# Keys and first query halves projected in one step for pairs 16 to 31, and 27 low parts computed on GpSimd

## The chip, the cores and the metric

The kernel runs on one core of a Trainium2 chip. The metric is the device time of one execution in microseconds (us). TensorE (PE in the profile) multiplies, VectorE (DVE), ScalarE (ACT) and GpSimd (POOL) do elementwise work, and every bulk transfer is issued from SyncE (SP). Results of TensorE land in eight banks of PSUM, each 512 float32 wide in 128 partitions; DVE and ACT read them from there.

## The reference

Attention with positive random features, followed by a gated feed-forward layer. There are 8 batches of 8 heads with 576 tokens and head width 64:

```python
def phi(x):
    proj = einsum('bhsd,df->bhsf', x, w_phi)              # 64 -> 128 features
    proj = proj - max(abs(proj), axis=-1)
    return concatenate([exp(proj), exp(-proj)], axis=-1)  # 256 features
q_p, k_p = phi(q), phi(k)
kv  = einsum('bhsf,bhsd->bhfd', k_p, v);  z = sum(k_p, axis=2)
x   = einsum('bhsf,bhfd->bhsd', q_p, kv) / (einsum('bhsf,bhf->bhs', q_p, z) + 1e-6)
g   = x @ w_gate                                          # 4608 x 512 @ 512 x 1536
out = (g / (1 + exp(-g)) * (x @ w_val)) @ w_out           # back to 4608 x 512
```

All tensors are float32. Two heads make a pair, so the attention has 32 pairs (0 to 31), four to a batch.

## The kernel before

**Feed-forward.** The 4608 tokens are twelve chunks of 384, the 1536 hidden columns twelve tiles f of 128. Every operand of these matmuls is split into a high part and a low part (the rest), and a product is the sum of three matmuls: high by high, high by low, low by high. `first(c, f)` makes one hidden tile of chunk c from the tokens, `second` multiplies a hidden tile into three blocks of outputs. A hidden tile ("middle tile", `m` in the trace) is either used at once or stored and fetched again later. Before `second` uses it, `parts` splits it: ACT copies the high part (`s4`, into a buffer `hh`) and another engine subtracts it from the tile to get the low part (`s5`). Chunk 0 is computed first while the weights are still being split on DVE, ACT and POOL (`weight_piece`, tiles `shared`, `ahead`, `w_big`, `w_hi`, `w_lo`). Then come chunks 1 to 3, during which POOL also makes sums of weights (`sums`, tile `s`), and chunks 4 to 11 go two at a time by a Strassen-like scheme (`strassen`, line 1145). The list `more_low` is empty until chunk 3 has been through `first`; `ring_on` is empty until chunks 1 to 3 are done.

**Attention.** `attention(i, rank)` adds the work of pair i: the keys are projected (lines 544 and 547: 8 matmuls into two banks and one, the tail, into a third), DVE takes the largest magnitude and subtracts it (lines 555, 561), ACT takes both exponentials (line 566), and 72 matmuls sum keys by values (lines 583, 576; called kv below). From pair 12 on the queries are projected in two halves of 288 columns, two matmuls each (line 689, called q below), ACT copies them out (line 694), DVE turns them and finds their maxima. Line 734 and line 743 then make denominators and numerators (called dn below).

**What sets the order.** All of this is a list of steps with costs, dependencies and ranks. `Plan.run` plays the list through with these costs and emits the instructions in the order in which the play starts them, so every engine's queue is written out beforehand. A step can take banks (`take`) and give them back (`give`); it starts in the play only when as many banks are free. The products of the feed-forward form one chain on PE. Attention work on PE of pairs 12 and up is ordered by due times, brought forward by `MARGIN`. [...] Where the play finds nothing ready for PE, it emits a filler matmul of 128 by 256 on zeros (`idle`, line 1342 before the first tile of the feed-forward, line 1344 after). PE steps have a mode: `rows` (64-row matmuls: key and query projections), `quarters` (32-column matmuls: kv and dn) and `whole`; once in a mode, the play goes on with steps of that mode that are ready.

## Time and profile before

| | us |
|---|---|
| Median of 3 runs | 1177.37 (1176.76 to 1177.45) |
| Profiled execution | 1175.58 |
| Span of the profiled execution | 1173.8 |
| PE busy in the span | 1161.7 (99%) |
| DVE busy | 829.4 (71%) |
| ACT busy | 594.7 (51%) |
| POOL busy | 139.1 (12%) |

[...] Matmuls overlap: the busy time of one is longer than the distance from its start to the start of the next, so what a step costs on PE is read from starts. The timeline merges consecutive instructions of one kind into a row with a count; the float32 matmuls of the attention appear in it as two passes each.

### The profile page before, as it was taken

Reading aid. Unit: us, or ns where it says so; the run is one execution under the profiler, and the core shown is the slowest. Engines: PE = TensorE matmul, PEld = TensorE weight load, DVE = VectorE, ACT = ScalarE, POOL = GpSimd, SP = SyncE. Lnnn points to the kernel's source line nnn. Section 1 sums busy time; section 2 is a strip of 40 time slices with the busy share of each in tenths; the row PEclk is TensorE's granted clock in tenths of the full one; section 3 lists DMA queues with packets and bytes.
Section 4 is the critical chain, followed back from the end, with each engine's and each line's share of the span. In section 5 each row is a group of like instructions: output and inputs, shape, how many; then the busy total and the mean of one; then the engine's idle time right before and its main releaser. Section 6 shows DMA issues by size and latency. Waiting matters only on the chain.

```text
span 1173.8 us, 29868 instructions
## 1 busy us (share of the span) xinstructions
PE 1161.7 (99%) x11684; PEld 995.1 (85%) x11684; DVE 829.4 (71%) x1509; ACT 594.7 (51%) x1325; POOL 139.1 (12%) x143
## 2 busy tenths in 40 slices
PE   9999999999999999999999999999999999999998
PEld 7777799999988877888887789887799878899986
DVE  7989999999646787768889475788645785534441
ACT  6887643333533657546665544566533654423332
POOL 1223210000032131101010001010001010001100
PEclk9999999999999999999999999999999999999999
DMA  5646789997698799897887689788779868789764
GB/s 169 179 123 180 247 267 302 308 294 256 221 335 283 243 325 365 301 307 233 275 290 240 219 281 303 231 250 249 260 231 302 255 198 276 276 272 306 253 217 160
DMA packets 217644, 301.68 MB, mean 257 GB/s; under 512 B 62752, under 2 KB 122272, under 8 KB 217504
## 3 DMA queue, kind: packets, MB, share of 16 engines
q1 hardware_dynamic: 217344, 299.71, 79.4%
q8 instruction: 92, 1.51, 0.5%
q14 instruction: 48, 0.39, 0.1%
q10 hardware_dynamic: 160, 0.07, 0.0%
HBM read 221.05 MB, written 78.64 MB: 255 GB/s over the span
## 4 chain that ended last, share of the span: by engine, by line
PE 90%; DVE 5%; DMA 1%; issue 1%; ACT 1%; SPq 1%; POOL 0%; DVEq 0%; ACTq 0%; POOLq 0%
PE work L382 39%; PE work L1145 31%; PE work L583 4%; PE work L743 4%; PE work L544 3%; PE work L689 2%; PE work L576 1%; PE work L662 1%; PE work L734 1%; DMA m<-h_dram 1%; PE work L1344 1%; PE work L739 1%; PE work L640 1%; PE work L1342 1%; DVE kp L561 1%
## 5 line engine op out<-in xcount | busy, mean ns | idle before, releaser
L382 PE MATMUL work<-w_hi,hh 128*128 128x512 f32 x468 | 183.0, 399 | 0.8 <-ACT osb L969 0.5
L1167 DVE TENSOR_TENSOR m<-m,work 128x384 f32<-128x384 f32 x144 | 78.6, 553 | 117.6 <-ACT m L1164 68.0
L382 PE MATMUL work<-w_hi,m 128*128 128x512 f32 x396 | 156.6, 396 | 0.0
L382 PE MATMUL work<-xh,w_big 128*128 128x384 f32 x384 | 132.0, 344 | 1.7 <-DVE m L911 1.7
L375 DVE TENSOR_TENSOR m<-m,hh 128x384 fp32r<-128x384 f32 x132 | 74.4, 570 | 79.7 <-ACT hh L938 75.6
L382 PE MATMUL work<-xl,w_big 128*128 128x384 f32 x384 | 128.6, 335 | 0.0
L938 ACT CAST hh<-m 128x384 fp32r<-128x384 f32 x144 | 72.9, 512 | 109.6 <-PE work L382 62.9
L375 POOL TENSOR_TENSOR m<-m,m 128x384 f32<-128x384 f32 x48 | 58.0, 1208 | 590.7 <-DVE m L1172 423.9
L1145 PE MATMUL work<-tb,stream_xh 128*128 128x384 f32 x618 | 115.7, 338 | 0.1
L1145 PEld LDWEIGHTS work<-tb,stream_xh 128*128 128x128 f32 x618 | 107.1, 188 | 5.6 <-issue 3.5
L382 PEld LDWEIGHTS work<-w_hi,hh 128*128 128x128 f32 x468 | 87.8, 188 | 26.7 <-issue 4.5
L1164 ACT COPY m<-work 128x384 f32<-128x384 f32 x144 | 67.9, 474 | 68.8 <-PE work L1145 66.8
L566 ACT ACTIVATE kp<-kp 128x512 f32<-128x512 f32 x128 | 77.7, 627 | 34.0 <-DVE kp L561 32.9
L1171 ACT ACTIVATE m<-m 128x384 f32<-128x384 f32 x96 | 45.4, 517 | 89.1 <-DVE m L1167 89.0
L382 PEld LDWEIGHTS work<-w_hi,m 128*128 128x128 f32 x396 | 74.4, 188 | 18.2 <-DVE m L375 0.3
L1145 PE MATMUL work<-tb,stream_xl 128*128 128x384 f32 x468 | 87.8, 337 | 0.1
L1145 PEld LDWEIGHTS work<-tb,stream_xl 128*128 128x128 f32 x468 | 81.1, 188 | 3.3 <-issue 1.5
L382 PEld LDWEIGHTS work<-xh,w_big 128*128 128x128 f32 x384 | 72.3, 188 | 8.8 <-issue 3.8
L1145 PE MATMUL work<-tb,tb 128*128 128x384 f32 x408 | 77.6, 337 | 0.0
L583 PEld LDWEIGHTS work<-vf,kp 128*32 128x32 f32 x4096 | 61.9, 109 | 16.3 <-issue 12.5
L375 POOL TENSOR_TENSOR s<-s 128x256 f32<-128x256 f32 x48 | 40.9, 853 | 278.4 <-DMA s<-w_dram 221.6
L382 PEld LDWEIGHTS work<-xl,w_big 128*128 128x128 f32 x384 | 72.2, 188 | 1.0
(142 smaller groups left out, 2390.0 us busy)
## 6 DMA issues: line engine op xcount, KB each, us to landing
stream_xh<-wv_dram SPq DMA_DIRECT2D x103, 256.0 KB, 4.0
h_dram<-m SPq DMA_DIRECT2D x124, 192.0 KB, 3.9
m<-h_dram SPq DMA_DIRECT2D x124, 192.0 KB, 4.3
w_lo<-wlo_dram SPq DMA_DIRECT2D x80, 256.0 KB, 4.6
stream_xl<-wv_dram SPq DMA_DIRECT2D x78, 256.0 KB, 4.0
tb<-wv_dram SPq DMA_DIRECT2D x77, 256.0 KB, 4.0
stream_w_lo<-wv_dram SPq DMA_DIRECT2D x52, 256.0 KB, 3.8
stream_xl<-wlo_dram SPq DMA_DIRECT2D x48, 256.0 KB, 3.7
```

The costliest lines, as they stand in the source:

```text
L375: (nc.gpsimd if on == "POOL" else nc.vector).tensor_tensor(out=o, in0=a, in1=b, op=op)
L382: nc.tensor.matmul(o, l, r, start=a, stop=z)
L544: nc.tensor.matmul(work[plan.bank["k", i, h]][:, t * NF:(t + 1) * NF], kin[rows(h)[0], t * P:(t + 1) * P], wst[rows(h)[0]], start=True, st ...
L566: nc.scalar.activation(kpv[:, :m2, s], kpv[:, :m2, 1], AF.Exp, scale=-1.0 if s else 1.0)
L583: nc.tensor.matmul(ps_kv()[r, (2 * s + h) * VD:(2 * s + h + 1) * VD], kpv[:, t, s, r], vf[:, t, h], start=t == 0 and h + s == 0, stop=False)
L689: nc.tensor.matmul(work[plan.bank[keys[h]]][:, :SH], wst[rows(h)[0]], qin[jq][rows(h)[0], c], start=True, stop=True)
L743: nc.tensor.matmul(o[at:at + 32], kvs[j][:, k * P + at:k * P + at + 32], features(k, at // D, c), start=first_ and k == 0, stop=k == 1)
L938: s4 = add("ACT", act(CH), lambda: nc.scalar.copy(hh[b], th(j)), [made, hid_free[b]], FIRST)
L1145: nc.tensor.matmul(o(), l, r, start=begin and k + m == 0, stop=k + m == 3, skip_group_check=True)
L1164: return j, into(j, add("ACT", act(CH), lambda: nc.scalar.copy(th(j), src()), after, FIRST))
L1167: return add("DVE", dve(CH), lambda: vec.tensor_tensor(out=th(j), in0=th(j), in1=src(), op=ALU.add), after, FIRST)
L1171: s1 = into(t, add("ACT", act(CH), lambda: nc.scalar.activation(th(t), th(j), AF.Tanh, scale=0.5), [ready], FIRST))
```

## The change

For pairs 16 to 31 (`joint`) one step on PE projects the keys, the tail of the keys and the first half of the queries. It takes four banks together: two for the keys, two for the queries, and the tail lies in the first query bank behind the query's 288 columns. That bank is given back only when both ACT has copied the queries and DVE has subtracted from the tail. The second half of the queries stays a step of its own and waits for the joint one. `MARGIN` goes from 65e3 to 75e3. In `parts`, the low part of a tile is made on POOL and no longer on DVE as long as `more_low` and `ring_on` are empty, which is so for 27 tiles: the twelve of chunk 0 and the first fifteen of chunks 1 and 2.

```diff
-MARGIN = 65e3
+MARGIN = 75e3
...
+        joint = i >= 16
...
+            tail_bank, tail_at = (("k", i, 2), slice(0, NF)) if not joint else (("q", i, 0, 0), slice(SH, SH + NF))
...
                 if both or not early:
-                    nc.tensor.matmul(work[plan.bank["k", i, 2]][:, :NF], kin[:D, 4 * P:], wst[:D], start=True, stop=True)
+                    nc.tensor.matmul(work[plan.bank[tail_bank]][:, tail_at], kin[:D, 4 * P:], wst[:D], start=True, stop=True)
+                if joint:
+                    for h in range(2):
+                        nc.tensor.matmul(work[plan.bank["q", i, h, 0]][:, :SH], wst[rows(h)[0]], qin[jq][rows(h)[0], :SH],
+                                         start=True, stop=True)
...
-                kproj = add("PE", (4 if early else 5) * pe32(NF), project, [*k_in, last.get(("kp", i - 1, 0))], rank,
-                            take=[("k", i, n) for n in range(2 if early else 3)], mode="rows")
+                kproj = add("PE", (4 if early else 5) * pe32(NF) + (pe32(SH) if joint else 0), project, [
+                    *k_in, last.get(("kp", i - 1, 0)), *((*q_in, *use("qx"), last.get(("qy", 3 * i - 1))) if joint else ())], rank,
+                            take=[("k", i, n) for n in range(2 if early or joint else 3)] + ([("q", i, h, 0) for h in range(2)] if joint else []), mode="rows")
...
-            ksub = add("DVE", dve(n), centre, [kmax, last.get(("kp", i - 1, g))], rank, give=key)
+            ksub = add("DVE", dve(n), centre, [kmax, last.get(("kp", i - 1, g))], rank, give=None if both and joint else key)
...
-                pj = add("PE", pe32(SH), project, [*q_in, *use("qx"), last.get(("qy", 3 * i - 1))], rank, take=keys, mode="rows")
+                pj = add("PE", pe32(SH), project, [*q_in, *use("qx"), last.get(("qy", 3 * i - 1)), *([kproj] if joint else [])], rank, take=keys, mode="rows") if part or not joint else kproj
...
+            if joint:
+                add("PE", 1, lambda: None, [copies[0][0], ksub], -2.0, give=("q", i, 0, 0))
...
-        s5 = pair_op("DVE2", CH, low, lambda: th(j), lambda: hh[b], ALU.subtract, [s4], FIRST)
+        s5 = pair_op("POOL" if not ring_on and not more_low else "DVE2", CH, low, lambda: th(j), lambda: hh[b], ALU.subtract, [s4], FIRST)
```

**PE, the projections of pair 17, between products of chunk 3.** Before, both halves of its queries are one stretch (four matmuls of line 689), followed by 18 filler matmuls and the dn of an earlier pair:

```order
L382 MATMUL work_135<-w_hi_79,m_5658 128x512
L689 MATMUL work_137<-qin,wst 128x288
L689 MATMUL work_134<-qin,wst 128x288
L689 MATMUL work_133<-qin,wst 128x288
L689 MATMUL work_130<-qin,wst 128x288
L1344 MATMUL work_132<-idle 128x256 x18
L734 MATMUL work_131<-num,ones 32x288 x2
L734 MATMUL work_131<-den,ones 32x288 x2
L743 MATMUL work_131<-qe_108,kvs_104 32x64 x4
```

In the changed kernel the same pair's step ends with the last matmuls of the keys, the tail (line 551) and two query matmuls (line 554), the tail and a query half in one bank:

```order
L548 MATMUL work_133<-wst,kin 128x128
L548 MATMUL work_131<-wst,kin 128x128
L551 MATMUL work_130<-wst,kin 128x128
L554 MATMUL work_130<-qin,wst 128x288
L554 MATMUL work_136<-qin,wst 128x288
L382 MATMUL work_134<-w_hi_79,hh_122 128x512
L382 MATMUL work_134<-w_lo_85,hh_122 128x512
L382 MATMUL work_134<-w_hi_79,m_5602 128x512
```

The products of the same weight tile (`w_hi_79`) now follow directly, without filler between.

**DVE, in the weight phase, behind one hidden tile of chunk 0** (the row that writes it is the first; `ahead` and `shared` are pieces of weights). Before, DVE makes the tile's low part two instructions later:

```order
L914 TENSOR_TENSOR m_3211<-m_3211,work_131 128x384
L375 TENSOR_TENSOR ahead<-shared_129,w_big_71 128x512
L375 TENSOR_TENSOR hh_122<-m_3211,hh_120 128x384
L409 TENSOR_SCALAR shared_128<-shared_128 128x512
L411 TENSOR_SCALAR shared_128<-shared_128 128x512
L413 SCALAR_TENSOR_TENSOR shared_129<-shared_127,shared_128 128x512
L416 TENSOR_SCALAR shared_128<-shared_129 128x512
```

Now:

```order
L925 TENSOR_TENSOR m_3205<-m_3205,work_131 128x384
L416 TENSOR_SCALAR shared_128<-shared_129 128x512
L418 SCALAR_TENSOR_TENSOR shared_128<-shared_126,shared_128 128x512
L375 TENSOR_TENSOR shared_129<-shared_129,shared_128 128x512
L409 TENSOR_SCALAR shared_128<-shared_128 128x512
L411 TENSOR_SCALAR shared_128<-shared_128 128x512
L375 TENSOR_TENSOR ahead<-shared_129,w_big_71 128x512
```

The row with `hh` is gone from DVE, and rows on weights follow one another.

**POOL, from the end of the weights to the sums of weights.** Before, after the last piece of weights nothing stands in POOL's queue until the sums (`s`):

```order
L375 TENSOR_TENSOR ahead<-shared_129,w_hi_75 128x512
L375 TENSOR_TENSOR shared_129<-shared_129,shared_128 128x512
L375 TENSOR_TENSOR ahead<-shared_129,w_big_70 128x512
L375 TENSOR_TENSOR s_4110<-s_4110 128x256 x4
L375 TENSOR_TENSOR s_4111<-s_4111 128x256 x4
```

Now the low parts (`hh` for chunk 0, `m` for chunks 1 and 2) stand there, some of them behind sums that wait for their own load:

```order
L375 TENSOR_TENSOR hh_123<-m_4027,hh_121 128x384
L375 TENSOR_TENSOR m_4133<-m_4133,hh_120 128x384
L375 TENSOR_TENSOR m_4138<-m_4138,hh_121 128x384
L375 TENSOR_TENSOR m_4145<-m_4145,hh_122 128x384
L375 TENSOR_TENSOR m_4152<-m_4152,hh_123 128x384
L375 TENSOR_TENSOR s_4185<-s_4185 128x256 x4
L375 TENSOR_TENSOR s_4186<-s_4186 128x256 x4
L375 TENSOR_TENSOR m_4376<-m_4376,hh_120 128x384
L375 TENSOR_TENSOR s_4185<-s_4185 128x256 x2
L375 TENSOR_TENSOR m_4422<-m_4422,hh_121 128x384
```

27 rows with low parts have come to POOL in all, and none has left it.

## Rows read from the trace of the kernel before

**Rows 1.** The page: busy time of PE with its share of the span and its instructions, and the chain of work that ended last, by engine.

```profile
PE 1161.7 (99%) x11684; PEld 995.1 (85%) x11684; DVE 829.4 (71%) x1509; ACT 594.7 (51%) x1325; POOL 139.1 (12%) x143
...
PE 90%; DVE 5%; DMA 1%; issue 1%; ACT 1%; SPq 1%; POOL 0%; DVEq 0%; ACTq 0%; POOLq 0%
```

**Rows 2.** What PE waited for, longest first: us in total, times, longest.

```profile
PE work L382 <- DVE m L911: 1.7, 2, 1.2
PE work L1339 <- POOL vl L357: 1.6, 1, 1.6
```

**Rows 3.** Filler matmuls after the first tile, grouped by line: count, busy us, mean ns.

```profile
L1344 PE MATMUL work<-idle 128*128 128x256 f32 x99 | 14.9, 287 | 0.0
```

**Rows 4.** Timeline of PE around steps in `rows` mode: start and duration in us, line, count. First one half of a pair's queries alone, then both halves together, then the keys of a pair, each with the matmul before and behind it.

```profile
363.37 0.34 PE L382 MATMUL work<-xh,w_lo1v 128*128 128x384 f32 x1
363.63 0.76 PE L689 MATMUL work<-qin,wst 64*128 64x288 f32 x4
364.32 0.44 PE L382 MATMUL work<-xh,w_big 128*128 128x384 f32 x1
...
427.76 1.24 PE L689 MATMUL work<-qin,wst 64*128 64x288 f32 x8
428.93 0.74 PE L1344 MATMUL work<-idle 128*128 128x256 f32 x4
...
434.04 0.40 PE L382 MATMUL work<-w_hi,m 128*128 128x512 f32 x1
434.37 1.16 PE L544 MATMUL work<-wst,kin 64*128 64x128 f32 x16
435.37 0.38 PE L547 MATMUL work<-wst,kin 64*128 64x128 f32 x2
435.68 0.50 PE L382 MATMUL work<-w_hi,hh 128*128 128x512 f32 x1
```

**Rows 5.** Timeline of PE around steps in `quarters` mode: kv alone, dn alone, and dn and kv together, first instruction of each and the first one behind it.

```profile
378.93 2.02 PE L583 MATMUL work<-vf,kp 128*32 128x65 f32 x128
...
381.32 0.44 PE L382 MATMUL work<-xh,w_big 128*128 128x384 f32 x1
...
391.43 0.44 PE L734 MATMUL work<-num,ones 128*32 128x288 f32 x2
...
394.00 0.45 PE L382 MATMUL work<-xh,w_big 128*128 128x384 f32 x1
...
417.00 0.44 PE L734 MATMUL work<-num,ones 128*32 128x288 f32 x2
...
421.82 0.44 PE L382 MATMUL work<-xh,w_big 128*128 128x384 f32 x1
```

**Rows 6.** Timeline of PE at the two longest filler runs, near the end of chunk 3, with the instruction behind each; then ACT's copy of the high parts for the products behind the second run (two copies merged).

```profile
472.80 2.40 PE L1344 MATMUL work<-idle 128*128 128x256 f32 x18
475.13 0.44 PE L734 MATMUL work<-num,ones 128*32 128x288 f32 x2
...
481.21 2.18 PE L1344 MATMUL work<-idle 128*128 128x256 f32 x17
483.23 0.40 PE L382 MATMUL work<-w_hi,hh 128*128 128x512 f32 x1
...
480.61 0.93 ACT L938 CAST hh<-m 128x384 fp32r<-128x384 f32 x2
```

**Rows 7.** Busy time by stretch of 15 us: length, then PE, PEld, DVE, ACT, POOL busy us (instructions), granted clock, DMA share, GB/s.

```profile
425.00:440.00 15.00, 14.82 (x103) 10.75 (x104) 10.84 (x18) 6.44 (x15) 3.18 (x5) 1.00 1.00 335
...
455.00:470.00 15.00, 15.00 (x199) 12.15 (x198) 11.43 (x18) 11.24 (x20) 0.72 (x1) 1.00 1.01 360
```

**Rows 8.** The same view in the weight phase, two stretches of one weight tile each.

```profile
201.00:217.30 16.30, 16.30 (x92) 15.26 (x91) 15.61 (x31) 6.37 (x13) 0.00 (x0) 1.00 0.89 292
217.30:233.50 16.20, 16.20 (x104) 15.22 (x103) 14.94 (x28) 5.29 (x9) 0.00 (x0) 1.00 0.91 306
```

**Rows 9.** DVE's groups by line with their mean ns, first from 90 to 180 us, where POOL ran 17 instructions, then from 180 to 270 us, where it ran none.

```profile
L411 DVE TENSOR_SCALAR shared<-shared 128x512 uint32<-128x512 uint32 x11 | 8.0, 724 | 0.2
L409 DVE TENSOR_SCALAR shared<-shared 128x512 f32<-128x512 f32 x11 | 5.8, 530 | 0.5 <-ACT shared L408 0.5
L375 DVE TENSOR_TENSOR hh<-m,hh 128x384 fp32r<-128x384 f32 x3 | 2.6, 874 | 0.0
...
L411 DVE TENSOR_SCALAR shared<-shared 128x512 uint32<-128x512 uint32 x16 | 6.8, 423 | 0.2
L409 DVE TENSOR_SCALAR shared<-shared 128x512 f32<-128x512 f32 x16 | 6.8, 423 | 1.9 <-ACT shared L408 1.9
L375 DVE TENSOR_TENSOR hh<-m,hh 128x384 fp32r<-128x384 f32 x5 | 2.8, 553 | 0.3 <-ACT hh L938 0.3
```

**Rows 10.** POOL's group of the same shape as a low part (another product of tiles), count, busy us, mean ns; and the first sums in POOL's timeline with the idle time before them.

```profile
L375 POOL TENSOR_TENSOR m<-m,m 128x384 f32<-128x384 f32 x48 | 58.0, 1208 | 590.7 <-DVE m L1172 423.9 <-DMA h_dram<-m 64.3 <-issue 36.5
...
321.31 7.33 POOL L375 TENSOR_TENSOR s<-s 128x256 f32<-128x256 f32 x8 [165.75 <-DMA s<-w_dram]
```

**Rows 11.** The first low part of chunks 1 and 2 on DVE, and the matmul on PE that uses it.

```profile
316.43 0.56 DVE L375 TENSOR_TENSOR m<-m,hh 128x384 fp32r<-128x384 f32 x1 [0.34 <-ACT hh L938]
...
318.76 0.39 PE L382 MATMUL work<-w_hi,m 128*128 128x512 f32 x1
```

More of the change, by code (lines that the diff above doesn't have):

```diff
@@ L536, in attention, with project @@
             key = ("k", i, g)
+            tail_bank, tail_at = (("k", i, 2), slice(0, NF)) if not joint else (("q", i, 0, 0), slice(SH, SH + NF))
             view = lambda key=key, n=n: work[plan.bank[key]][:, :n].rearrange("p (t f) -> p t f", f=NF)
-            def project(t0=t0, t1=t1, key=key, heads=heads, both=both):
+            if both:
+                view = lambda tail_bank=tail_bank, tail_at=tail_at: work[plan.bank[tail_bank]][:, tail_at].rearrange("p (t f) -> p t f", f=NF)
+            def project(t0=t0, t1=t1, key=key, heads=heads, both=both, tail_bank=tail_bank, tail_at=tail_at):
                 projected.append(1)
@@ L690, in project @@
                                          start=True, stop=True)
-                pj = add("PE", pe32(SH), project, [*q_in, *use("qx"), last.get(("qy", 3 * i - 1))], rank, take=keys, mode="rows")
+                pj = add("PE", pe32(SH), project, [*q_in, *use("qx"), last.get(("qy", 3 * i - 1)), *([kproj] if joint else [])], rank, take=keys, mode="rows") if part or not joint else kproj
                 for h in range(2):
                     copies[h].append(add("ACT", act(SH), lambda h=h, c=c, key=keys[h]: nc.scalar.copy(
-                        qx[j][:, h, c], work[plan.bank[key]][:, :SH]), [pj, *use("qx")], rank, give=keys[h]))
+                        qx[j][:, h, c], work[plan.bank[key]][:, :SH]), [pj, *use("qx")], rank, give=keys[h] if h or part or not joint else None))
+            if joint:
+                add("PE", 1, lambda: None, [copies[0][0], ksub], -2.0, give=("q", i, 0, 0))
             last["qin", i] = pj
```

## Prediction

> **What bounds the kernel now.** I read the page first: PE is busy for 1161.7 us of a span of 1173.8, and 90% of the chain that ended last is work on PE [rows 1]. What PE waited for comes next: the longest sum is 1.7 us [rows 2]. So there is hardly a wait to remove. The time is the sum of what PE executes, and a change pays by shortening that queue: fewer instructions, fewer fillers, fewer changes between the modes. The printed order says how many of each there are, and starts in PE's timeline say how long each takes. Third, I looked for stretches in which another engine only just keeps up, since fillers hide such waits. There are two. In the weight phase DVE works 15.61 of 16.30 us and 14.94 of 16.20 [rows 8]. Near the end of chunk 3 the transfers run at a share of 1.00 with 335 to 360 GB/s [rows 7].
>
> **Query and key steps, late pairs.** One query half alone occupies PE from 363.63 to 364.32, 0.69 us; two halves together take 427.76 to 428.93, 1.17 us, so the second costs 0.48. Keys with their tail take 434.37 to 435.68, 1.31 us [rows 4]. The joint step isn't in the trace. From below it costs 1.31 + 0.48 = 1.79 us, if the query half joins as a second half does; from above 1.31 + 0.69 = 2.00, if nothing is saved. I take 1.80, because both cases in the rows are one uninterrupted stretch in the same mode. Before, the order has 31 key steps alone, 28 query halves alone and 6 doubles; now 15, 24 and none, and 16 joint steps. That is 16 x 1.80 - 16 x 1.31 - 4 x 0.69 - 6 x 1.17 = -1.9 us (+1.3 with the upper end). Entering such a stretch from an ordinary matmul costs about 0.09 us more (363.37 to 363.63 is 0.26 where the usual distance is 0.17; 434.04 to 434.37 is 0.33 for 0.23) [rows 4]. I count 97 entries into `rows` or `quarters` stretches in both orders, so this term is zero.
>
> **kv and dn.** The joint steps use all the banks that the Strassen part leaves, so other steps are cut apart. kv alone takes 378.93 to 381.32, 2.39 us; dn alone 391.43 to 394.00, 2.57; both in one stretch 417.00 to 421.82, 4.82 [rows 5]. A cut costs 2.39 + 2.57 - 4.82 = 0.14 us. For pairs 12 and up 12 joined stretches become 9: +0.4 us. In the early pairs the order has four more cuts, in kv, dn and query steps. At 0.14 to 0.2 us, estimated from the same difference, and with slightly more for the transposes between them, that is +0.8 us.
>
> **Fillers.** There are 99 after the first tile before [rows 3] and 68 now. In a run one takes (483.23 - 481.21) / 17 = 0.119 us [rows 6]; the mean of 287 ns in the group counts overlapping time and would be wrong here. 31 x 0.119 = -3.7 us. The sum is -1.9 + 0.4 + 0.8 - 3.7 = -4.4 us.
>
> A filler that goes is worth its time only if PE would have had work. Most of those that go stand near the end of chunk 3: 40 of the 99 stand between 428 us and the Strassen part, and 16 are left in the same part of the chain of products. The rows tell how much was a real wait. The second run lasts from 481.21 to 483.23, but the copy of the high part for the next product ends at 480.61 + 0.93 = 481.54 [rows 6]. So at most 0.33 of its 2.02 us was needed. The first, 472.80 to 475.13, is followed by dn and not by a product; for it I can only say that between nothing and all of 2.33 was needed. Needed in the two runs: 0.33 to 2.66 of 4.35 us, 8 to 61%. On the 24 x 0.119 = 2.9 us that go here this gives back 0.2 to 1.8 us. I take 0.8, nearer to the run whose end I can see.
>
> **Low parts on GpSimd.** On DVE one costs 0.55 us when POOL is idle [rows 9]; on POOL an instruction of that shape takes 1.21 us [rows 10], 0.65 later at the user. The least cover that I found is at 316.43: the part ends at 316.99 and PE uses it at 318.76, 1.8 us later [rows 11]. So 0.65 is hidden. In chunks 1 and 2 the parts now stand in POOL's queue behind sums that wait for a load, and behind these the next parts wait; the sums' loads move ahead a little in SP's queue too, so I cost this at zero, and without that cover a late load would hold a part by several us.
>
> In the weight phase POOL was idle for 165.75 us up to 321.31 [rows 10], so there's room. But DVE gets slower beside POOL. With POOL at work the shift on line 411 takes 724 ns instead of 423, line 409 takes 530 instead of 423, the low part 874 instead of 553 [rows 9]: 11 x 0.30 + 11 x 0.11 + 3 x 0.32 = 5.5 us over 17 POOL instructions, 0.32 each. Eight of chunk 0's tiles fall in the stretch from 185 us where DVE only just keeps up, five of them up to 270 us [rows 9]. Each takes 0.55 off DVE and puts on between nothing and 1.21 (DVE held for the whole instruction), so DVE's work there changes by -4.4 to +5.3 us; at 0.32 it is 8 x (0.32 - 0.55) = -1.8. Against that the order brings attention work of DVE forward into this stretch. I take zero for PE and keep +5.3 as the upper end.
>
> [...]
>
> **Sum.** -4.4 + 0.8 = -3.6 us. The profiled execution goes from 1175.58 to 1172.0 (span 1173.8 to 1170.2); it lies 1.8 under the median of the runs, so against the median of 1177.37 I forecast 1173.8.
>
> **The rivals.**
> 1. *The fillers covered waits.* PE's queue gets shorter, but transfers at a share of 1.00 [rows 7] and DVE in the weight phase set the pace, and what was filler becomes idle time in front of line 382. For it: rows 7 and 8. Against it: the filler run that outlasted its data by 1.7 us. Then the 3.7 us come back: -0.7 us, 1176.7.
> 2. [...] Place: the weight phase, 185 to 316 us, where POOL was idle. Each of eight low parts meets a DVE instruction with two inputs and holds it for 1.21 us, DVE falls behind by 5.3 us, and some three us of attention work that now stand there (an estimate: the rows that the order adds, most of them of 0.3 to 1.3 us) can't be absorbed. Price +5.3 + 3.0 - 1.3 (the PE work that came with it) = +7.0, so -4.4 + 7.0 = +2.6: 1180.0. It decides when a low part costs DVE over about 1.2 us; the rows show 0.32.
> 3. *The joint step waits for banks.* It needs four at once, and in the Strassen part only four exist for attention. The second half comes 15 to 33 ordinary matmuls behind it in the printed order, and the tail's bank needs DVE to be done. If DVE is late by half a us at each of 16 pairs, PE stands 8 us: 1181.8. Against it: PE's longest waits name no line of the attention [rows 2], though there the tail had a bank of its own.
> 4. *More gain.* The wait of 1.7 us on line 911 [rows 2] goes as well since DVE has 0.55 less per tile, and no filler was needed: -4.4 - 1.7 = -6.1, 1171.3.
>
> **How the numbers follow.** Forecast 0.52, with a range of its own of 1171.5 to 1176 (the joint step's upper end and the two ends of what fillers give back, and a us for waits that fall elsewhere in a new order). Rival 1 has 0.20, rival 2 0.12, rival 3 0.07, rival 4 0.09. A measurement of this kernel tells about 0.2%, 2.35 us, from no change. Faster by more: nine tenths of the forecast, all of rival 4 and a little of rival 1, 0.58. Within: most of rival 1 and the rest of the forecast, 0.23. Slower: rivals 2 and 3, 0.19. The range is 1169.5 to 1180: below it only rival 4 with more of PE's waits gone, above it rival 3 and the worse part of rival 2.
>
> **What would show it.** Right: 68 fillers in the group of line 1344, with a busy time near 10 us; joint steps that last about 1.80 us from the first key matmul to the next ordinary matmul; query halves alone at 0.69; idle sums on PE no longer than before; low parts of `hh` and `m` in POOL's groups at about 1.2 us. Wrong: idle time before line 382 or 1145 of some us, released by POOL (rival 2 or a part behind a late sum), by DVE's lines 561 or 555 (rival 3) or by transfers (rival 1); or lines 409 and 411 at a mean far over 423 ns between 180 and 270 us.

## The result: 0.57% slower, and the profile after

The changed kernel takes 1183.44 us (median of 8 runs, 1179.74 to 1185.81), the kernel before in the same comparison 1176.72 (8 runs, 1173.89 to 1179.85): a ratio of 1.0057, 95% interval 1.0044 to 1.0071. The forecast was 1173.8 in a range of 1169.5 to 1180.0. The profiled execution took 1179.74 us (span 1177.9), against 1175.58 before. It is the fastest of the eight: the loss that its trace can explain is 4.2 us, the loss of the medians is 6.7.

The page of the changed kernel: span, busy time of each engine, the queues of kind `instruction`, and the chain that ended last.

```profile
span 1177.9 us, 29815 instructions
PE 1157.9 (98%) x11653; PEld 989.5 (84%) x11653; DVE 819.0 (70%) x1482; ACT 594.7 (50%) x1325; POOL 163.7 (14%) x170
...
q8 instruction: 92, 1.51, 0.5%
q14 instruction: 48, 0.39, 0.1%
...
PE 92%; DVE 3%; DMA 2%; issue 1%; SPq 1%; ACT 1%; DVEq 0%; ACTq 0%
```

PE is busy 3.8 us less than in [rows 1], in a span 4.1 us longer. So PE stands more. What it waited for (sum in us, times, longest):

```profile
PE work L585 <- issue: 3.8, 4, 1.6
PE work L1156 <- issue: 2.7, 1, 2.7
PE work L382 <- DVE m L922: 2.4, 3, 1.0
PE work L745 <- issue: 1.7, 1, 1.7
PE work L1350 <- POOL vl L357: 1.6, 1, 1.6
PE work L754 <- issue: 1.4, 1, 1.4
PE work L1156 <- DVE m L1178: 1.0, 1, 1.0
```

Line 922 is line 911 of before, where [rows 2] have 1.7 us, and line 1350 is line 1339, with 1.6. The wait on line 1178 is new. What stands out are the four rows whose releaser is "issue": PE waits for nothing that the profile shows, for 9.6 us. They stand at three unrelated steps: kv, the Strassen part, dn. The kernel before has two such rows, which [rows 2] leave out:

```profile
PE work L576 <- issue: 1.2, 2, 0.9
PE work L544 <- issue: 0.5, 1, 0.5
```

The terms of the prediction did come out. The group of late fillers, which answers to [rows 3]:

```profile
L1355 PE MATMUL work<-idle x68: 274/282/384, 206.0 to 1122.3; 128*128 128x256 f32 x68
```

And a joint step in PE's timeline (start, duration, tile, shape), which answers to [rows 4]:

```profile
433.94 1.16 PE L548 MATMUL work<-wst,kin 64*128 64x128 f32 x16
434.94 0.27 PE L551 MATMUL work<-wst,kin 64*128 64x128 f32 x1
434.94 0.51 PE L554 MATMUL work<-qin,wst 64*128 64x288 f32 x1
435.05 0.27 PE L551 MATMUL work<-wst,kin 64*128 64x128 f32 x1
435.16 0.65 PE L554 MATMUL work<-qin,wst 64*128 64x288 f32 x3
435.74 0.50 PE L382 MATMUL work<-w_hi,hh 128*128 128x512 f32 x1
```

From 433.94 to 435.74 it takes 1.80 us, as forecast, and all 16 joint steps take 1.79 or 1.80. So the loss isn't in the steps that the change makes. It lies in stand-stills like these two, in the timeline of the changed kernel (in brackets the idle time before the row and its releaser):

```profile
389.91 2.02 PE L592 MATMUL work<-vf,kp 128*32 128x65 f32 x128
391.75 0.62 PE L585 MATMUL work<-vl,kpt 128*32 128x130 f32 x14
393.79 0.41 PE L585 MATMUL work<-vl,kpt 128*32 128x130 f32 x2 [1.42 <-issue]
...
586.39 0.68 PE L1156 MATMUL work<-tb,stream_w_lo1v 128*128 128x384 f32 x3
589.75 1.14 PE L1156 MATMUL work<-tb,stream_w_lo1v 128*128 128x384 f32 x3 [2.67 <-issue]
```

The kv step of 389.91 stops after 14 of the 16 last matmuls; a row of six equal matmuls of line 1156 is cut in the middle. Nothing in the program separates the first part from the second. What separates them is their number. I counted all the trace's records of PE's queue in order of time (weight loads, matmuls and the few records of semaphores; without these the remainder below does not come out) and set beside each stand-still the last packet of queue q8 (kind `instruction`, 92 packets of 16 KB):

```
number of    = 256 x  PE starts  next     gap    packet of q8        next start
the record            last at    start           from      to       after the packet
 4800        18 + 192   110.06    111.84   1.79   109.52   110.48    1.36
 6080        23 + 192   156.67    157.14   0.47   154.76   155.74    1.40
 9664        37 + 192   392.10    393.80   1.70   391.55   392.47    1.32
14016        54 + 192   586.75    589.75   3.01   587.50   588.38    1.37
15296        59 + 192   640.80    642.76   1.95   640.47   641.51    1.25
17600        68 + 192   769.94    772.06   2.12   769.66   770.61    1.46
18880        73 + 192   823.73    824.62   0.89   822.33   823.27    1.35
```

All seven lie at a number that leaves 192 over 256, and PE goes on 1.25 to 1.46 us after a packet has come. Together they are 11.93 us. The kernel before has three of this kind, 2.44 us in all. I take the places to be the edges of the pieces in which PE's program is fetched, 256 instructions in 16 KB. Both figures are in the trace (1.51 MB in 92 packets; stand-stills at distances that are multiples of 256). In order of time, each of the trace's 92 such numbers after the first has its own packet among the 92, and at none of these 91 does PE pass sooner than 1.25 us after the end of that packet, also where it doesn't stand.

In this trace, how long PE stands follows from two things: how fast it runs through the piece before the edge, and when the packet for the next piece starts. In the median a packet starts 0.7 us after PE has passed the edge before it and lasts 1.0 us. Five of the seven pieces were run through in 1.8 to 2.3 us. The other two (the stand-stills at 586.75 and 640.80) took 3.1 and 3.5 us, but their packets started 3.8 and 3.2 us after the edge before; why so late the trace doesn't say.

The longest has a sequel. Busy time per stretch of the changed kernel (columns: stretch, length, busy us and instructions of PE, PEld, DVE, ACT, POOL, granted clock, DMA share, GB/s):

```profile
583.00:586.70 3.70, 3.70 (x152) 3.25 (x151) 3.70 (x6) 2.25 (x7) 1.21 (x1) 1.00 0.91 292
586.70:589.80 3.10, 0.43 (x4) 0.11 (x2) 2.83 (x9) 0.43 (x2) 0.00 (x0) 1.00 1.10 368
589.80:593.40 3.60, 3.60 (x34) 2.56 (x38) 2.61 (x2) 0.00 (x0) 0.00 (x0) 0.53 0.59 184
593.40:597.00 3.60, 3.60 (x27) 2.14 (x20) 0.49 (x1) 1.41 (x5) 0.00 (x0) 1.00 0.04 9
```

PE stands, and then its granted clock is 0.5 of full speed for 3.41 us by the trace's clock records (590.0 to 593.4), so some 1.7 us of work are lost (an estimate: half of the 3.41). The first row shows the other side: before the stand-still PE ran 152 matmuls in 3.70 us, while the transfers were at 0.91 to 1.10 of their share.

The account of the profiled executions: the sum as forecast -3.6, edges 11.93 - 2.44 = +9.5, the clock +1.7, which makes +7.6; measured +4.2. The other 3.4 us went the right way, and the experiments come back to them. Of the 2.5 us by which the medians differ more, part may be the clock: its mean is 0.998 of full speed in the profiled execution and in one other, and 0.996 or 0.997 in the other six. A mean lower by 0.001 to 0.002 over 1178 us is 1 to 2.4 us (an estimate from these means; there is no trace of those executions).

### The profile page after: what moved, and what is told of

Read it like the earlier page. It is cut to its first block, busy times and chain, and to the rows that moved or that the text cites. A ratio compares the mean times of both kernels' runs of the same rounds, so it can differ in the third digit from the quotient of the medians.

```text
span 1177.9 us, 29815 instructions
## 1 busy us (share of the span) xinstructions
PE 1157.9 (98%) x11653; PEld 989.5 (84%) x11653; DVE 819.0 (70%) x1482; ACT 594.7 (50%) x1325; POOL 163.7 (14%) x170
## 3 DMA queue, kind: packets, MB, share of 16 engines
q8 instruction: 92, 1.51, 0.5%
## 4 chain that ended last, share of the span: by engine, by line
PE 92%; DVE 3%; DMA 2%; issue 1%; SPq 1%; ACT 1%; DVEq 0%; ACTq 0%
PE work L382 39%; PE work L1156 30%; PE work L754 5%; PE work L592 5%; PE work L548 3%; PE work L698 1%; PE work L585 1%; PE work L750 1%; PE work L745 1%; PE work L671 1%; PE work L649 1%; PE work L554 1%; DMA kin<-in_kT_dram 1%; DMA shared<-in_wv_dram 1%; PE work L1353 1%
## 5 line engine op out<-in xcount | busy, mean ns | idle before, releaser
L375 DVE TENSOR_TENSOR m<-m,hh 128x384 fp32r<-128x384 f32 x117 | 65.4, 566 | 76.6 <-ACT hh L949 73.0
L1156 PEld LDWEIGHTS work<-tb,tb 128*128 128x128 f32 x408 | 70.7, 188 | 4.5 <-issue 3.2
```

What stands on the lines that cost most here:

```text
L375: (nc.gpsimd if on == "POOL" else nc.vector).tensor_tensor(out=o, in0=a, in1=b, op=op)
L1156: nc.tensor.matmul(o(), l, r, start=begin and k + m == 0, stop=k + m == 3, skip_group_check=True)
```

## Experiments

**Theory.** PE stands where a burst of short matmuls (kv: 288 instructions in 2.4 us) runs it over the edge of a piece before the next piece is there. The change moved the instructions against the edges, and more bursts fell on one. **Rivals.** The joint step waits for banks, or DVE and POOL hold each other up in the weight phase (the prediction's rivals 3 and 2): then the place of the edges doesn't matter, and the changed kernel stays at its 1183 us wherever they lie.

**Moving the edges alone.** A number of tiny matmuls on zeros ahead of PE's first filler moves all later instructions against the edges and leaves the order of every queue as it is. PE has only fillers there anyway (20 of line 1339, from 1.57 to 6.01 us in the kernel before). 52 matmuls are 208 instructions; 18 are 72, 40 are 160, 54 are 216 and 64 are 256.

```diff
+    padded = []
     def nothing():
         if not begun and not projected:
+            if not padded:
+                padded.append(1)
+                zeros = idle.bitcast(F32)
+                for n in range(52):
+                    nc.tensor.matmul(ps(("gv", 1, 0), VD)[quarters[n % 4]], zeros[:, :32], zeros[:, :VD], start=True, stop=True)
```

The changed kernel with 208 instructions:

> The changed kernel with 208 more instructions in front of PE's first filler matmul (52 matmuls of 32 by 65 on zeros, in four instructions each), everything else in the same order. Theory (code fetch): PE's program comes in pieces of 256 instructions; in the changed kernel's trace PE stood six times, 11.5 us in all, each time at an instruction whose number is 192 modulo 256, and went on 1.2 to 1.5 us after a piece of 16384 bytes had landed. Moving the program by 208 instructions puts the bursts of attention matmuls elsewhere against the edges; by the times between edges in the trace some 4 to 8 us of the standing goes, the padding itself costs at most 1.5 us at the start: 1175 to 1180 against 1183.4. [...]

Measured: 1172.33 us (1169.92 to 1177.12), ratio to before 0.9963 (0.9944 to 0.9983). Eleven us less than without padding, and under the theory's own range.

With 72:

> The changed kernel with 72 more instructions in front (18 of the same matmuls). Theory (code fetch): by the times between edges this is near the worst place, 12 edges fall where PE runs through a piece in under 2.9 us instead of 6: 6 to 14 us slower than the changed kernel, 1189 to 1197. [...]

Measured: 1172.15 us (1171.1 to 1174.36), ratio 0.9965 (0.995 to 0.9979). The number that I had expected to be the worst place is as good as the other. So my forecast of single edges is no use: it went by how fast PE runs through a piece alone, and the start of the packet varies as well (in this kernel up to 5.8 us after the edge before); that the place decides stands. In PE's timeline of this kernel the kv step that stopped at 391.75 goes through:

```profile
389.31 2.02 PE L592 MATMUL work<-vf,kp 128*32 128x65 f32 x128
391.15 0.63 PE L585 MATMUL work<-vl,kpt 128*32 128x130 f32 x16
391.71 0.76 PE L698 MATMUL work<-qin,wst 64*128 64x288 f32 x4
```

The kernel before with 216 and with 160 instructions:

> The kernel before with 216 more instructions in front. Theory (code fetch): no edge is left where PE runs through a piece in under 2.9 us (4 now), so the kernel before gets 0 to 3 us faster less at most 1.5 us of padding: 1173 to 1177. Rivals, which speak of the change alone: 1177 to 1178.5.

Measured: 1180.45 us (1178.98 to 1183.12), ratio 1.0029 (1.0012 to 1.0046). A miss: I had expected a gain. The edges sum to 5.87 us in its profile. The longest stands in these rows of PE's timeline, and by the trace's clock records 6.8 us at 0.5 of the full clock begin in it (504.7 to 511.5; another 3.4 us of this execution, from 95.1, follow a wait of PE away from the edges):

```profile
500.28 2.00 PE L583 MATMUL work<-vf,kp 128*32 128x65 f32 x122
505.91 0.44 PE L583 MATMUL work<-vf,kp 128*32 128x65 f32 x6 [3.63 <-issue]
```

> The kernel before with 160 more instructions in front. Theory (code fetch): ten edges instead of four where PE runs through a piece in under 2.9 us: 6 to 14 us slower than before, 1183 to 1191, though no order, wait or engine changed. Rivals: padding alone, 1177 to 1178.

Measured: 1180.57 us (1180.17 to 1183.15), ratio 1.0035 (1.0022 to 1.0048), edges 7.95 us. That is some 2.5 us under the range of the theory and as much above that of the rivals. At both other places the kernel before is 3 to 4 us slower, so it owed as much to a lucky place of its edges.

**The control.** A whole piece of padding brings every instruction back to its place within a piece.

> The changed kernel, order of every queue as it is, with 64 tiny matmuls (256 instructions, one whole piece of PE's program) ahead of PE's first filler. Theory (PE stands where a burst of small matmuls runs it over the edge of a 256-instruction piece before the next has come): every later instruction lies where it lay within its piece, so the stand-stills come back: 1182 to 1186 us, edge gaps summing to 10 to 13 us in the profile, at the same steps as in the changed kernel (L585, L1156, L754, L745). Rival (the padding as such helps, for instance because PE is busy earlier, whatever its length): as with 72 and 208 instructions, 1171 to 1174 us.

Measured: 1184.56 us (1179.36 to 1186.36), ratio 1.0064 (1.0048 to 1.0081); edges 13.31 us, at the lines expected. The same padding code, three lengths: 1172, 1172 and 1184.6. So it isn't the padding that helps, it's the place. All four forecasts of single places had missed; this one, which asks for no length of a stand-still, holds.

**The cost by itself.** 512 tiny matmuls in one go.

> The same with 512 tiny matmuls (2048 instructions, eight pieces) in one go: the disputed cost measured by itself. Theory: within the burst PE stands once in every 256 instructions, at numbers that leave 192 over 256, with each stand-still 0.5 to 3 us and the next matmul 1.2 to 1.5 us after the end of a 16 KB packet of the instruction queue; the piece is run in some 2 us and comes in some 3, so that eight pieces take some 24 us rather than 16. The rest of the program keeps its phase, so it has the changed kernel's gaps. Rival (PE's code is there ahead of time and the stand-stills are a wait that the profile does not name): the burst runs through without a gap over 0.3 us. Total some 1185 to 1205 us, of no use by itself.

Its timeline on PE:

```profile
7.34 2.02 PE L1356 MATMUL work<-idle 128*32 128x65 f32 x128 [1.26 <-issue]
12.44 2.02 PE L1356 MATMUL work<-idle 128*32 128x65 f32 x128 [3.08 <-issue]
15.90 2.02 PE L1356 MATMUL work<-idle 128*32 128x65 f32 x128 [1.44 <-issue]
19.63 2.02 PE L1356 MATMUL work<-idle 128*32 128x65 f32 x128 [1.71 <-issue]
23.36 2.02 PE L1356 MATMUL work<-idle 128*32 128x65 f32 x128 [1.71 <-issue]
26.81 2.02 PE L1356 MATMUL work<-idle 128*32 128x65 f32 x128 [1.44 <-issue]
```

This is the clearest row of the study. There is no operand to wait for, and PE runs exactly 128 matmuls with their 128 weight loads and stops, each time. A piece is executed in 2.02 us and comes every 3.4 to 3.7 us (once 5.1). The packets in this stretch last 0.96 to 1.56 us and PE goes on 1.40 to 1.53 us behind each. Total 1203.75 us.

**GpSimd's low parts.** The order stays, the low parts are issued on VectorE at the same place. Done with 72 instructions of padding, with none and with 208.

```diff
-    def pair_op(on, n, out, in0, in1, op, after, rank):
+    def pair_op(on, n, out, in0, in1, op, after, rank, issue=None):
...
-            (nc.gpsimd if on == "POOL" else nc.vector).tensor_tensor(out=o, in0=a, in1=b, op=op)
+            (nc.gpsimd if (issue or on) == "POOL" else nc.vector).tensor_tensor(out=o, in0=a, in1=b, op=op)
...
-        s5 = pair_op("POOL" if not ring_on and not more_low else "DVE2", CH, low, lambda: th(j), lambda: hh[b], ALU.subtract, [s4], FIRST)
+        s5 = pair_op("POOL" if not ring_on and not more_low else "DVE2", CH, low, lambda: th(j), lambda: hh[b], ALU.subtract, [s4], FIRST, "DVE")
```

> The changed kernel with the 72 instructions of padding, and the low parts that the change gave to GpSimd issued on VectorE at the same place of the order (PE's queue is instruction for instruction the same). Compare with 1172.2 us for the padding alone. Theory (GpSimd's low parts cost and bring next to nothing): 1171 to 1174 us. [...] Other rival (the low parts on GpSimd are what the gain is from, VectorE being late for PE): 1175 to 1180 us.

Measured: 1170.88 us (1168.83 to 1171.69), ratio 0.9947 (0.9935 to 0.9959); 1172.15 with the low parts on GpSimd. This is faster than both kernels. PE's waits for hidden tiles and low parts, first with the low parts on GpSimd (72 instructions of padding), then on VectorE, 2.0 and 1.0 us:

```profile
PE work L382 <- DVE m L922: 1.7, 2, 1.0
PE work L382 <- POOL m L375: 0.3, 1, 0.3
```

```profile
PE work L382 <- DVE m L925: 0.6, 1, 0.6
PE work L382 <- DVE m L922: 0.4, 1, 0.4
```

> The changed kernel without padding, its 27 low parts issued on VectorE at the same place of the order; PE's queue instruction for instruction that of the changed kernel. Theory (the place of the 256-instruction edges makes the loss, and GpSimd's low parts cost some 1.3 us, as with 72 instructions of padding): 1180.5 to 1184 us, edge gaps 10 to 14 us. [...]

Measured: 1182.05 us (1176.28 to 1187.32), ratio 1.0039 (1.0021 to 1.0057), edges 15.11 us. Without padding most of the loss stays (0.39% of 0.57%) though GpSimd does no low part. So what DVE and POOL cost each other isn't its cause.

> The changed kernel with 208 instructions of padding (1172.3 us) and its low parts on VectorE: whether the 1.3 us found with 72 is there at another place of the edges too. If the low parts on GpSimd cost: 1170 to 1171.5 us. If that was chance of the edges: 1172 to 1174 us.

Measured: 1174.26 us (1168.68 to 1177.4), ratio 0.9974 (0.9956 to 0.9993). By time this contradicts the run with 72; its profile has edges of 12.59 us and a half-clock stretch, against 8.30 and none with the low parts on GpSimd. The edges scatter by more than what I wanted to measure.

**The parts alone.** Each part sets a new order, and so a new place of the edges. The joint step alone is the changed kernel with two lines set back:

```diff
-MARGIN = 75e3
+MARGIN = 65e3
...
-        s5 = pair_op("POOL" if not ring_on and not more_low else "DVE2", CH, low, lambda: th(j), lambda: hh[b], ALU.subtract, [s4], FIRST)
+        s5 = pair_op("DVE2", CH, low, lambda: th(j), lambda: hh[b], ALU.subtract, [s4], FIRST)
```

The margin alone and GpSimd alone are the kernel before with the one or the other of these lines as the change has it.

> The joint step of four banks alone: the table's margin stays at 65e3 and all low parts stay on VectorE. The order of PE and so the place of the edges is a third one. Terms of the prediction: the joint step brings 1.9 us and the fillers' 3.7 us hang on the whole; the edges may add or take 5 to 10 us. By the theory the time is 1174 us plus (edge gaps in its profile minus 2.4 us) plus any half-clock stretch's half: the sum, not the time, is what I expect within 2 us. By the rivals (banks of the joint step late, a loss of the step itself) time stays 1179 to 1184 us with edge gaps under 5 us.

Measured: 1174.48 us (1173.32 to 1181.06), ratio 0.9988 (0.9972 to 1.0003). Edges 5.23 us, so 1176.8 was expected within 2 us; it is 2.3 lower. It has 133 late fillers, 34 more than before.

> The kernel before with the table's margin of 75e3 alone (some fillers fewer, the burden of the joint step and of GpSimd left out). My prediction's term for the fillers was -3.7 us for 31 of them, all from the whole change; by theory the time is 1176.8 us minus 0.119 us for every filler fewer, plus the change of the edge gaps (2.4 us before) and half of a half-clock stretch. By the rival that fillers cover waits: no gain, and waits on DVE or ACT longer by what the fillers took.

Measured: 1180.5 us (1177.84 to 1183.9), ratio 1.0034 (1.002 to 1.0047), 94 fillers, edges 4.20 us in the profiled run of 1178.27. That run is where the theory has it (1176.8 - 0.6 + 1.8 = 1178.0); the median is 2.5 above, for which I have no profile.

> The kernel before with the low parts on GpSimd alone (the table set anew with them). Theory: within 1.5 us of 1176.8 us plus the change of the edge gaps (2.4 us before) and half of a half-clock stretch. [...]

Measured: 1176.62 us (1174.24 to 1181.46), ratio 1.0001 (0.9986 to 1.0016), 85 fillers, edges 8.80 us and 3.41 us at half the clock. Expected by the theory 1176.8 + 6.4 + 1.7, within 1.5: it is 8 below. So something here brings several us that I hadn't counted.

**What is left without the edges.** For each profiled execution: its time, less the gaps over 0.45 us at numbers 192 over 256, less half of its half-clock stretches.

```
                                   time     edges   half clock   rest
before                            1175.58    2.44      0        1173.1
before, 216 of padding            1183.12    5.87    10.24      1172.1
before, 160                       1180.67    7.95     3.41      1171.0
margin alone                      1178.27    4.20      0        1174.1
joint step alone                  1173.79    5.23      0        1168.6
GpSimd alone                      1177.82    8.80     3.41      1167.3
changed                           1179.74   11.93     3.41      1166.1
changed, 256                      1179.36   13.31     3.41      1164.3
changed, 208                      1170.31    8.30      0        1162.0
changed, 72                       1172.15    7.14      0        1165.0
changed, low parts on VectorE     1179.72   15.11     6.83      1161.2
   the same, 208                  1176.30   12.59     3.41      1162.0
   the same, 72                   1170.88    9.19      0        1161.7
```

Times that differ by 13 us fall into three groups, the parts alone aside: 1171 to 1173 for the kernel before, 1162 to 1166 for the changed one, 1161 to 1162 with the low parts on VectorE. So the change without its edges is worth about 1172.1 - 1164.4 = -7.7 us, twice my -3.6 (the rest takes a stand-still off in full, also where another wait would have come anyway, so it is good to about 2 us). What the low parts on GpSimd cost isn't settled: with no padding, 208 and 72 the rests differ by 4.9, 0.0 and 3.3 us, and the medians by 1.4, -1.9 and 1.3.

**What a filler is worth.** My largest term. The late fillers of the kernel before and of the fastest one are made shorter in place. First to 64 columns:

```diff
-            nc.tensor.matmul(ps(open_sum[-1], 2 * NF), idle[:, :P], idle, start=False, stop=False)
+            nc.tensor.matmul(ps(open_sum[-1], 64), idle[:, :P], idle[:, :64], start=False, stop=False)
```

> The kernel before, each of its 99 late fillers cut from 256 to 64 columns (they add zeros either way); number and order of PE's instructions as before, so the 256-instruction edges stay. My prediction took 0.119 us of PE's time for a filler, nearly all of it time that the end of the kernel sees. If that holds, and a short one takes some 0.06 us (an estimate: half; no row has one): 99 x 0.06 = 6 us less, 1170 to 1173 us with edge gaps of 2 to 4 us. Rival (the fillers stand where PE would wait): 1175.5 to 1178 us, and the waits of PE on DVE, ACT or loads in the profile longer by some 5 us. Third case: the granted clock falls in stretches with short fillers, 1179 us or more.

> The fastest kernel so far (the change, 72 instructions of padding, low parts on VectorE: 1170.9 us) with its 68 late fillers cut to 64 columns. If fillers are real time: 68 x 0.06 = 4 us less, 1166 to 1168.5 us. If they cover waits: 1169.5 to 1172.5 us. If the clock falls without them: 1173 us or more.

Measured: 1176.33 us (ratio 1.0001, 0.999 to 1.0011) and 1169.67 (0.9949, 0.9935 to 0.9963). Inconclusive: a short filler still takes 0.106 us, (483.44 - 481.63) / 17 in the first one's timeline, and my estimate of 0.06 was wrong. The weight loads of 128 columns, which stayed, start 0.11 us apart in that trace, so they may set the pace; that was not tested apart. Then with 32 columns of weights in fp32:

> The kernel before, each of its 99 late fillers now a matmul of 32 x 65 (as in the burst, 0.016 us each in a row) rather than 128 x 256; the cut to 64 columns alone left a filler at 0.106 us, since its weight load of 128 columns sets its pace, and so told little. Count and order of PE's instructions are those of before. If a filler's 0.119 us is time of the kernel, as my prediction had it: 99 x 0.10 less some 2 us for changes of mode, -6 to -9 us: 1167 to 1171 us with edge gaps of 2 to 4 us. Rival (they cover waits): 1175 to 1178 us, with PE's waits on DVE, ACT or loads up by 5 us or more. Third case (a lower granted clock where PE now idles): 1179 us or more, with half-clock stretches at the old filler runs.

> The same with the 68 late fillers of the change with 72 instructions of padding and low parts on VectorE (1170.9 us). If fillers are real time: 68 x 0.10 less 1.5 us, -4 to -6 us: 1165 to 1167.5 us. If they cover waits: 1169 to 1172 us. If the clock falls: 1173 us or more.

Measured: 1183.69 us (1.0053, 1.0037 to 1.0069) and 1173.21 (0.9972, 0.996 to 0.9985). Also not what I meant: each filler became two matmuls of 0.06 us (198 in the group), so no time was saved and every later edge moved. The kernel before thus becomes 6.9 us slower; of its profiled run (1180.11) some 6 us lie at edges. At last with one matmul in bf16, to four quarters in turn:

```diff
+    turn = []
...
-            nc.tensor.matmul(ps(open_sum[-1], 2 * NF), idle[:, :P], idle, start=False, stop=False)
+            turn.append(1)
+            nc.tensor.matmul(ps(open_sum[-1], 64)[quarters[len(turn) % 4]], idle.bitcast(mybir.dt.bfloat16)[:, :32], idle.bitcast(mybir.dt.bfloat16)[:, :64], start=False, stop=False)
```

> The kernel before, each of its 99 late fillers a single matmul of 32 x 64 zeros in bf16, to the four quarters of the array in turn (in fp32 it became two matmuls, one after the other in one quarter, as long as the old filler, and moved the edges by two instructions each: the run with tiny fillers told about the edges again and not about fillers). Two instructions for a filler as before, so the edges stay. If the 0.119 us of a filler is time of the kernel: 99 x 0.08 to 0.10, less some 2 us for changes of mode: 1167 to 1171 us with edge gaps of 2 to 4 us. Rival (they cover waits): 1175 to 1178 us, with PE's waits up by 5 us or more. Third case (the clock falls): 1179 us or more, with half-clock stretches.

> The same with the 68 late fillers of the change with 72 instructions of padding and low parts on VectorE (1170.9 us). If fillers are real time: 1165 to 1167.5 us. If they cover waits: 1169 to 1172 us. If the clock falls: 1173 us or more.

Measured: 1174.74 us (1171.72 to 1177.63), ratio 0.9983 (0.9973 to 0.9994), and 1169.58 (1166.09 to 1174.72), ratio 0.9942 (0.9922 to 0.9962). PE's timeline of the first at the filler run of 481.21 in [rows 6], and its waits:

```profile
480.46 0.32 PE L1347 MATMUL work<-idle 128*32 128x64 bf16 x17
480.71 0.50 PE L382 MATMUL work<-w_hi,hh 128*128 128x512 f32 x1
481.05 0.40 PE L382 MATMUL work<-w_lo1v,hh 128*128 128x512 f32 x1
481.86 0.50 PE L382 MATMUL work<-w_hi,m 128*128 128x512 f32 x1 [0.41 <-DVE m L375]
```

```profile
PE work L382 <- DVE m L911: 3.4, 4, 1.4
PE work L382 <- DMA w_lo<-wlo_dram: 1.6, 1, 1.6
...
PE work L382 <- ACT hh L938: 0.9, 1, 0.9
```

A filler now takes 0.25 / 17 = 0.015 us, so 99 x (0.119 - 0.015) = 10.3 us are out of PE's queue. The time falls by 1.8 (0.7 to 3.2 by the interval). The rest is waits: line 911 3.4 us where [rows 2] have 1.7, a load of 1.6, the high part 0.9; distances over 0.6 us between starts away from the edges sum to 14.8 us, against 6.3 before. So about four fifths of the fillers' time stood where PE would have waited. Set side by side matmul by matmul, the two profiled executions agree: the distances behind fillers sum to 9.3 us less, all others to 9.1 more. The fastest kernel's fillers covered waits too: there the fillers give 6.3 us, and all other distances away from the edges take 6.1 back, much of it in waits of 0.1 to 0.3 us. But waits over 0.6 us are 4.4 us in it after the cut, 10 less than in the kernel before, and the times without edges are 1161.5 and 1172.7. So what the change gains is that these waits are gone, and not that fillers are; that kernel has its low parts on VectorE.

## Why the prediction was wrong

- **The step that failed** is "So there is hardly a wait to remove. The time is the sum of what PE executes". The sum has no term for where instructions lie against the edges of the fetched pieces. The trace of before already held three such stand-stills (2.44 us; in the list of PE's waits they have the releaser "issue", which I passed over). The changed kernel has seven, and with the clock that is +11.2 us of profiled time; 256 instructions of padding keep them (1184.6), 72 and 208 turn the loss into the gain (1172.2, 1172.3).
- **The joint step** was right: 1.80 us at each of 16 pairs, and 68 fillers as counted.
- **Fillers.** The count was right, but 0.119 us for each isn't time by itself. I took 0.8 of 2.9 us as needed, from the one run of fillers whose end I could see, at most 0.33 of 2.02 us. There the reading was near: with short fillers 0.41 us of idle time came back. But that run doesn't stand for the others: of all 99, about 82% is needed (8.5 of 10.3 us). That the term came out with its sign is luck: the waits went with the fillers, which the sum had no reason for. The gain without the edges, about -7.7, is larger than -3.6; in the two kernels with quarter fillers it lies in waits over 0.6 us that are gone. How it divides among the three parts stays open: the rest of the parts alone is -3.5 for the joint step, -4.8 for GpSimd, +2.0 for the margin, each with an order of its own.
- **Low parts on GpSimd**, costed at zero: 0.32 us for DVE beside each POOL instruction was too small. In the changed kernel's groups of DVE from 180 to 270 us (count, busy us, mean ns, idle before), where POOL now runs six low parts, four groups have means of 783, 738, 735 and 475 ns. In the same stretch of before, where POOL ran nothing, they have 690, 690, 688 and, in [rows 9], 423. That is 3.6 us more in all:

```profile
L375 DVE TENSOR_TENSOR shared<-shared,shared 128x512 f32<-128x512 f32 x15 | 11.7, 783 | 0.4
L418 DVE SCALAR_TENSOR_TENSOR shared<-shared,shared 128x512 f32<-128x512 uint32 x15 | 11.1, 738 | 0.4
L413 DVE SCALAR_TENSOR_TENSOR shared<-shared,shared 128x512 uint32<-128x512 uint32 x15 | 11.0, 735 | 0.2
L411 DVE TENSOR_SCALAR shared<-shared 128x512 uint32<-128x512 uint32 x16 | 7.6, 475 | 0.3
```

A mean hides what happens here. Five of the six low parts each hold one DVE instruction, by 0.69 to 0.81 us, and the other instructions of these groups keep their time. One such meeting, DVE and POOL (start, duration):

```profile
196.37 1.24 DVE L411 TENSOR_SCALAR shared<-shared 128x512 uint32<-128x512 uint32 x1
196.21 1.11 POOL L375 TENSOR_TENSOR hh<-m,hh 128x384 fp32r<-128x384 f32 x1 [14.40 <-ACT hh L949]
```

Over the eight low parts from 185 us on, DVE loses 4.8 us, 0.60 for each, and is spared 8 x 0.55 = 4.4. So DVE gains nothing in the stretch where it only just keeps up; I had -1.8 there. What this costs the kernel is open, as said above: 1.3 us by time with 72 of padding, nothing to be seen with 208.

- **Rivals.** 1: its premise holds (fillers do cover waits), its outcome doesn't (in the fastest kernel the waits went too). 2: DVE is held by up to 0.82 us at a meeting, 0.60 in the mean, and not by its 1.21; but that is not the cause, since most of the loss stays without it. The held instruction above ends 0.29 us after POOL's. What it loses, 0.81 us, is under the 0.95 us that POOL's has left when it starts, and so under the 1.21 that I took for DVE held through a whole instruction of POOL. So the mean of 0.32 said little about a single meeting. What makes DVE wait for POOL there, no run shows. 3: no wait of PE names banks or the tail, and the joint step alone is not slower. 4: its 1171.3 lies near the 1172.2 with 72 of padding, but by luck: the wait on line 922 is still there, 1.7 us with 72 and 2.4 without, and most of the fillers' time was needed. I gave the true cause no chance at all.

## What to carry to other kernels

Before a change of a fraction of a percent is judged on a program of many thousand short instructions, move its edges: a few tens of harmless matmuls ahead of the first work showed 11 us here, more than the change itself. With 72 instructions of them and the low parts back on VectorE the changed order is 0.5% faster than the kernel before. In the profile, waits on "issue" in the middle of a run of one kind of matmul were the sign (9.6 us of them in the changed kernel); count the instructions up to them. And look twice at a mean when two engines may hold each other up: a few long instructions among many of the usual length tell more. Fillers were for the most part waits in disguise here (8.5 of 10.3 us): their number didn't say what their removal would bring.

## What the runs showed of the hardware

- In the changed kernel 91 of the 92 packets of 16 KB in queue q8 went one by one with edges in PE's queue, one every 256 instructions, and PE stood at seven of them. After a stand-still PE went on 1.21 to 1.61 us after a packet's end in all runs. In the burst of 512 tiny matmuls a piece, 2.02 us of work, came every 3.4 us or more, so that PE was idle two fifths of the time.
- Two stand-stills of 3 us came with a granted clock of 0.5 of full speed: the 3.01 us at 586.75 in the changed kernel with 3.41 us of it, the 3.63 us at 502 in the kernel before with 216 of padding with 6.8 us. After the gaps of 0.5 to 2.1 us listed above, and in the first 30 us of the burst with its 3.08 us, the clock was 1.00.
- In a run of fillers, a matmul of 64 columns against 128 columns of weights took 0.106 us, of 256 columns 0.119, so the number of columns was not most of it; the weight load may be (not tested apart). In bf16, against 32 columns of weights and to four quarters in turn, 64 columns took 0.015 us.
- A low part on POOL (1.0 to 1.5 us) held one DVE instruction by 0.69 to 0.82 us at seven of nine meetings of the weight phase from 180 us on; the other instructions of those lines kept their time.
